# Down products of a transformer block by Strassen's rule, with keys read twice into short rings

## The chip, the cores and the metric

The kernel runs on one core of a Trainium2 chip. Its engines are PE (TensorE, matrix products into PSUM, an accumulation memory of eight banks), DVE (VectorE), ACT (ScalarE), POOL (GpSimd, which works on SBUF, the on-chip memory, alone) and SP (SyncE, which issues DMAs). Each works through its own queue in order; semaphores join them. The metric is the time of one execution in microseconds (us) on the device: the median of several runs.

## What is computed

The reference is a gated pair of transformer branches over 2048 tokens of width 576 (float32):

```python
def _A_ref(x, wqkv, wo):                    # 32 heads of 18
    ...
    scores = jnp.einsum("bhqd,bhkd->bhqk", q, k) * (Dh ** -0.5)
    p = _softmax(scores, axis=-1)
    o = jnp.einsum("bhqk,bhkd->bhqd", p, v)
    return (lambda x, *d: x.transpose(*d))(o, 0, 2, 1, 3).reshape(B, S, D) @ wo

def _B_ref(x, w_gate, w_up, w_down):        # hidden width 4608
    return (_gelu(x @ w_gate) * (x @ w_up)) @ w_down

xn = _layernorm(x, axis=-1)
s = _A_ref(xn, A_wqkv, A_wo)
g = _silu(_B_ref(xn, B_w_gate, B_w_up, B_w_down))
return x + s * g
```

## The kernel before

**Numbers.** Most products are made of float32 operands cut into a high part (rounded to fp32r) and a low part (the rest), with three terms: high x high, high x low, low x high. `split` (L105) cuts on POOL: one one-input operation for the high part, one two-input operation for the low part.

**Stages.** A prologue normalizes x, projects q, k and v and stores them to DRAM (`qk`, `vs`). Then the feed-forward branch runs with the attention woven in; an epilogue ends the feed-forward branch and makes the output projection.

**Feed-forward.** Tokens come in 4 blocks of 512, the hidden width in 36 tiles of 128. One `section` (L644) makes gate and up of one hidden tile for one token block: 27 pairs of matmuls (`gate_up`, L488), gate in the upper and up in the lower 64 rows of the array, then `activate` (L508) makes the hidden tile from the two PSUM banks `pg`, `pu` (ACT: a square, a copy, a tanh; DVE: three operations, the last one `rest`), and `finish` (L692) splits it on POOL. Two sections are a **round** (r of 18 in a block): after its second section the down weights of the two tiles are split too (`dh`, `dl`), and in the next section's tail `downs` (L686) makes the round's down products.

**Down products.** 512 tokens are 4 tiles of 128, 576 columns are 2 halves of 288: eight sums of 2 hidden tiles x 3 terms = 6 products of 128 rows each. In the attention stage `half_downs` (L570) makes each as two products of 64 rows, the upper and the lower half side by side as pairs, in an order written out by hand over eight banks. `add_down` (L542) adds each finished sum to `Y` on DVE. In the last rounds (L633) the products use 128 rows.

**Attention.** A unit is 4 heads by 512 queries: 32 units, 4 sections each. The scores are computed twice: first for the maxima (`max_mm`, L805, reduced by DVE), 40 slots ahead, then for the exponentials (`score_mm`, L858, ACT). Each section has 8 slots of two pairs (`slot_pairs`, L874), spread between its gate and up pairs. After each second section `values` (L892) multiplies exponentials by values, so a round of two sections holds one burst of value products. Four small operations of DVE a unit (`max_neg`, L823) and DMAs (`max_rows`, L849) turn the maxima into rows of q. The keys lie in `KS`, a ring of 7 chunks of 512 keys, each with two tiles of two heads; maxima and scores read the same copy. `load_k` (L768) fills a chunk by 12 DMAs of 18 rows. PSUM's eight banks are three rings: `m` (3), `s` (3), `f` (2).

**Weights.** `load_gu` (L122) loads a hidden tile's gate and up weights by two DMAs, `split_gu` (L129) cuts them in three pieces into rings of five (`wh`, `wl`).

**Order.** PE runs in the order of the text. The other engines' orders are laid by a planner, except where `keep_in_program_order` (through `kept`, from the epilogue on) or an ordering edge (`no_sync`) pins them. All DMAs are issued by SP.

Of the kernel before, what the change touches and what calls it, by code (L numbers as in the profile page):

```python
# [17 lines left out]
P = 128  # L18
# [18 lines left out]
KB, VB = 7, 2  # L37
LEAD = NS + SLOTS
G = 2
# [3 lines left out]
ATT = range(len(FIRST), len(FIRST) + NU * NA)  # L43
MROW = 3 * DH
# [25 lines left out]
def kernel(ctx: ExitStack, tc: tile.TileContext, x, wqkv, wo, w_gate, w_up, w_down, out):  # L70
# [32 lines left out]
    low_part, asked, copied = [], [], []  # L103
# [15 lines left out]
    def raw_tile(shape, pool=wts):  # L119
        return pool.tile(shape, F32, name="raw", tag="raw", bufs=2)  # L120

    def load_gu(t, keep=lambda i: i):  # L122

        raw = raw_tile([P, NC, P])
        for a, w in enumerate((w_gate, w_up)):
            keep(nc.sync.dma_start(raw[HR * a:HR * a + HR], w[:, t * P:(t + 1) * P].rearrange("(k p) n -> p k n", p=HR)))
# [9 lines left out]
    def load_xd(b, key=None):  # L136

        xd = [[], []]
        for c in range(0, NC, XG):
            for i in range(2):  # L140
# [3 lines left out]
                if key:  # L144
                    no_sync(asked[0], key, "keys first")
                copied[:] = [nc.gpsimd.tensor_copy(t[HR:P], t[0:HR])]
                xd[i].append(t)
        return xd
# [5 lines left out]
    with tc.tile_pool(name="pro", bufs=1) as pro, tc.tile_pool(name="pps", bufs=1, space=PSUM) as pps:  # L154
        ident = pro.tile([P, P], F32, name="ident")
        make_identity(nc, ident)

        def load_rest(c0, n, keep=lambda i: i):

            raw = raw_tile([P, n])  # L160
# [199 lines left out]
        def split_wo(k):  # L360
            n = min(P, D - k * P)
            raw = raw_tile([P, D])
# [75 lines left out]
        for b in range(NB):  # L438
# [37 lines left out]
    copied.clear()  # L476
    FF = {"w": ahead, "xd": XD, "down": [], "n": 0, "keep": None, "late": [], "marks": False, "between": [], "added": None,
          "Y": ffn.tile([P, TB // P, D], F32, name="Y")}
# [29 lines left out]
    def activate(pg, pu, early):  # L508

        t1 = ffn.tile([P, TB], F32, name="t1", bufs=2)  # L510
        FF["square"] = kept(nc.scalar.activation(t1, pg, AF.Square))
        one = kept(nc.vector.scalar_tensor_tensor(t1, t1, 1.0 / GC, pg, op0=ALU.add, op1=ALU.mult))
# [6 lines left out]
        def times(behind=None, _=None):  # L519
            one = nc.scalar.activation(t2, pu, AF.Copy)  # L520
            if behind:
                no_sync(one, behind, "a mark first")
            two = nc.vector.tensor_tensor(t2, t2, pg, op=ALU.mult)
# [3 lines left out]
        def tanh(behind=None, _=None):  # L527
            one = kept(nc.scalar.activation(t1, t1, AF.Tanh, scale=GC * GS))
# [3 lines left out]
        def rest(_=None, evicted=None):  # L532
            one = kept(nc.vector.scalar_tensor_tensor(t1, t1, 1.0, t2 if early else pg, op0=ALU.add, op1=ALU.mult))  # L533
# [8 lines left out]
    def add_down(b, r, py, Y, j, c):  # L542
# [101 lines left out]
    def section(specials=(), tag="f", raw_d=None, ahead=True):  # L644
# [6 lines left out]
        if g == 0:  # L651
            FF["hs"] = []
# [535 lines left out]
```

## Time and profile before

| | |
|---|---|
| median of 3 runs | 2535.45 us (2535.36 to 2535.55) |
| span of the profiled execution, first to last instruction | 2533.5 us |
| granted TensorE clock, mean | 1.000 |
| PE / DVE / ACT / POOL busy | 2526.7 / 1953.2 / 1562.0 / 1330.1 us |
| HBM read and written | 266.63 and 54.70 MB |

The profile is of one execution; about 2 us of the time lie around its span. Its page gives busy times, the chain of work that ended last, and the costliest groups of instructions as "line engine operation out<-in shapes xcount | busy us, mean ns | idle before". Other views list instructions in order of time ("start us, us, engine line ..."), or of one line with shortest, median and longest duration. "PEld" is the load of weights into the array, "SPq" is SP's issuing of DMAs, which no busy share counts. A shape such as 64*128 beside a matmul tells the rows and columns of the array that it uses.

### The profile page before, as it was taken

The numbers are of one execution on the slowest core, as the hardware profiler recorded it, in microseconds if no ns is written. First come the engines' busy times: TensorE is split into PE (matmuls) and PEld (weight loads), VectorE is DVE, ScalarE is ACT, GpSimd is POOL, SyncE is SP. The second block draws the span as 40 slices with busy tenths as digits, with TensorE's granted clock in tenths as the row PEclk, the third lists the DMA queues.
The fourth block names the chain that finished last, engine by engine and source line by source line (L and its number), as shares of the span: only waits on it lengthen the run. The fifth ranks groups of instructions, "written<-read, shape, count | busy, mean of one in ns | idle before, by whom it ended". The sixth has DMA issues, their size and how long they took to land.

```text
span 2533.5 us, 63814 instructions
## 1 busy us (share of the span) xinstructions
PE 2526.7 (100%) x24196; PEld 2011.3 (79%) x24196; DVE 1953.2 (77%) x3489; ACT 1562.0 (62%) x3099; POOL 1330.1 (53%) x1462
## 2 busy tenths in 40 slices
PE   9999999999999999999999999999999999999999
PEld 8899987777777778777777777777777777777798
DVE  5317988888888888888888888888888888887277
ACT  3223566676666676666766666766667666666622
POOL 4127554445565545544465555455446555555575
PEclk9999999999999999999999999999999999999999
DMA  7876434444464444444465444444447444444493
GB/s 243 284 263 161 103 94 107 110 111 115 102 156 110 108 112 104 110 113 114 113 135 141 106 111 106 110 104 104 116 110 162 104 106 107 110 111 95 113 250 107
DMA packets 397664, 325.54 MB, mean 128 GB/s; under 512 B 117408, under 2 KB 308160, under 8 KB 397360
## 3 DMA queue, kind: packets, MB, share of 16 engines
q1 hardware_dynamic: 397360, 321.47, 50.1%
q8 instruction: 193, 3.16, 0.6%
q14 instruction: 111, 0.91, 0.1%
HBM read 266.63 MB, written 54.70 MB: 127 GB/s over the span
## 4 chain that ended last, share of the span: by engine, by line
PE 100%; DVE 0%; DMA 0%; issue 0%; ACT 0%
PE pg L498 30%; PE py L561 18%; PE acc L901 18%; PE pm L813 9%; PE pe L866 9%; PE po L177 7%; PE pu L498 5%; PE po L1048 2%; PE pt L247 0%; DMA xx<-in_A_x_dram 0%; PE pt L258 0%; PE pt L177 0%; DVE bs L384 0%; DVE xx L213 0%; DVE yy L1055 0%; DVE yy L1056 0%
## 5 line engine op out<-in xcount | busy, mean ns | idle before, releaser
L867 ACT ACTIVATE pT<-pe 128x512 f32<-128x512 f32 x2048 | 1152.7, 598 | 368.8 <-PE pm L813 228.8
L816 DVE TENSOR_REDUCE mx<-pm 128x1 f32<-128x512 f32 x2048 | 1250.2, 680 | 147.7 <-PE pm L813 145.5
L498 PE MATMUL pu<-xd,wh 64*128 64x512 f32 x2592 | 926.9, 390 | 0.0
L498 PE MATMUL pg<-xd,wh 64*128 64x512 f32 x2592 | 925.8, 390 | 0.0
L813 PE MATMUL pm<-KS,q 64*128 64x512 f32 x2048 | 780.4, 388 | 0.0
L866 PE MATMUL pe<-q,KS 64*128 64x512 f32 x2048 | 777.3, 387 | 0.0
L498 PEld LDWEIGHTS pg<-xd,wh 64*128 64x128 f32 x2592 | 477.2, 184 | 111.8 <-POOL wh L106 29.3
L498 PE MATMUL pu<-xd,wl 64*128 64x512 f32 x1296 | 501.6, 387 | 0.0
L498 PE MATMUL pg<-xd,wl 64*128 64x512 f32 x1296 | 501.5, 387 | 0.0
L498 PEld LDWEIGHTS pu<-xd,wh 64*128 64x128 f32 x2592 | 477.3, 184 | 1.0
L901 PE MATMUL acc<-pT,VS 128*32 128x512 f32 x4096 | 452.8, 594 | 0.0
L108 POOL TENSOR_TENSOR wl<-raw,wh 128x384 fp32r<-128x384 f32 x432 | 434.0, 1018 | 14.0
L106 POOL TENSOR_SCALAR hh<-t 128x512 fp32r<-128x512 f32 x129 | 79.7, 618 | 649.8 <-DVE t L533 647.7
L813 PEld LDWEIGHTS pm<-KS,q 64*128 64x128 f32 x2048 | 375.2, 184 | 28.7 <-DVE mx L816 1.9
L866 PEld LDWEIGHTS pe<-q,KS 64*128 64x128 f32 x2048 | 372.5, 184 | 21.6
L901 PEld LDWEIGHTS acc<-pT,VS 128*32 128x32 f32 x4096 | 127.5, 110 | 289.7 <-issue 284.9
L561 PE MATMUL py<-dh,hh 64*128 64x288 f32 (+1 forms) x2240 | 353.5, 293 | 0.0
L561 PE MATMUL py<-dl,hh 64*128 64x288 f32 (+1 forms) x2240 | 352.7, 292 | 0.0
L561 PE MATMUL py<-dh,hl 64*128 64x288 f32 (+1 forms) x2240 | 352.5, 292 | 0.0
L106 POOL TENSOR_SCALAR wh<-raw 128x384 fp32r<-128x384 f32 x432 | 216.5, 513 | 197.8 <-PE pu L498 130.5
L498 PEld LDWEIGHTS pg<-xd,wl 64*128 64x128 f32 x1296 | 238.8, 184 | 31.2
L549 DVE TENSOR_TENSOR Y<-py,Y 128x288 f32<-128x288 f32 x544 | 226.4, 450 | 40.2 <-PE py L561 32.5
(146 smaller groups left out, 3105.4 us busy)
## 6 DMA issues: line engine op xcount, KB each, us to landing
KS<-qk SPq DMA_DIRECT2D x1536, 36.0 KB
raw<-in_B_w_gate_dram SPq DMA_DIRECT2D x144, 288.0 KB
raw<-in_B_w_up_dram SPq DMA_DIRECT2D x144, 288.0 KB
raw<-in_B_w_down_dram SPq DMA_DIRECT2D x67, 576.0 KB
VS<-vs SPq DMA_DIRECT2D x128, 152.0 KB
qk<-t SPq DMA_DIRECT2D x72, 256.0 KB
q<-qk SPq DMA_DIRECT2D x384, 36.0 KB
xx<-in_A_x_dram SPq DMA_DIRECT2D x32, 288.0 KB
```

What stands on the lines that cost most here:

```text
L106: first = nc.gpsimd.tensor_scalar(hi, raw, 1.0, 1.0, op0=ALU.mult, op1=ALU.mult)
L108: low_part[:] = [keep(nc.gpsimd.tensor_tensor(lo, raw, f(hi), op=ALU.subtract))]
L177: nc.tensor.matmul(o, st, m, start=(i == 0), stop=(i == len(TERMS) - 1))
L498: nc.tensor.matmul(o, w[1 + wp][k][rr, c, :], xd[xp][k][rr, c, :], start=(i == 0), stop=(i == len(terms) - 1))
L549: one = FF["added"] = kept(nc.vector.tensor_tensor(yy, py, yy, op=ALU.add))
L561: return nc.tensor.matmul(py, hs[g][a][rr, j * P:(j + 1) * P], wd[w][rr, g, 288 * c:288 * c + 288], start=start, stop=stop)
L813: nc.tensor.matmul(pm, QS[u, r][rr, t * P:(t + 1) * P], KS[(u * NA + c) % KB][r][rr, :], start=True, stop=True)
L816: return nc.vector.tensor_reduce(MX[u][:, 2 * r + a, t, c:c + 1], pm, axis=AX.X, op=ALU.max)
L866: nc.tensor.matmul(pe, KS[(u * NA + c) % KB][r][rr, t * P:(t + 1) * P], QS[u, r][rr, :], start=True, stop=True)
L867: nc.scalar.activation(PT[u, kt][:, 2 * r + a, :], pe, AF.Exp, scale=SCALE)
L901: nc.tensor.matmul(ACC[u][32 * a:32 * a + 32, :], VS[(u * NA + c) % VB][:, v:v + 32], pt[:, a, :], start=first, stop=last, skip_group_chec ...
L1048: nc.tensor.matmul(po, parts_of(b, j)[x_][:, k, :], OW[w][c][k], start=(i == 0), stop=(i == len(OUT) - 1))
```

## The change

In 63 rounds (5 to 67, `SEVEN`) the down products of a round, a product of 512 tokens x 256 hidden by 256 x 576, are made as seven products of blocks of half the size in each direction, by Strassen's rule in Winograd's form. `cut_hidden` and `cut_down` make the sums and differences of blocks and split them, on POOL, with the high parts of four weight blocks on ACT. `seven_downs` makes 7 products x 2 token tiles of 128 = 14 sums of 3 matmuls of 128 rows. The seven results are added up apart over all rounds of a block of tokens (`Y` has 7 places for each token tile); ten of the 14 sums go out on DVE, four on ACT into `TY`, which `add_copied` adds by two operations of DVE at the end of the round's second section. `combine` joins the seven into the four blocks by seven operations of DVE at the end of a block.

The ring of keys becomes two rings of 3 half chunks, `KM` for the maxima and `KS` for the scores, so that each key is read twice; the slots of a section go through the first half chunk and then the second. Gate and up weights come in three pieces of two DMAs, in one ring of six with the low parts; the high parts have a ring of four. Splits are pinned at thirds of a section. A block's transposed x is copied to the lower half on POOL and ACT, half each. The output projection's weights go to places that become free late, and are loaded later. Names that moved (`S3` to `SIDE`), the epilogue's order of splits, `load_wo` and the functions that only lost an argument are left out of the diff below.

```diff
-KB, VB = 7, 2
+KB, VB = 3, 2
 LEAD = NS + SLOTS
+LEAD_K = 2 * LEAD // SLOTS
+UNITS = 6
+NT_GU = 3 * XG
 G = 2
 NR = F // (G * P)
 NF = NB * NR * G
 FIRST = (0, 0) + (5,) * 8
 ATT = range(len(FIRST), len(FIRST) + NU * NA)
+SEVEN = range(ATT.start // G, ATT.stop // G - 1)
+HALF, CW = TB // 2, D // 2
+A12, A22, A11, S3, S2, S1, S4 = range(7)
+B11, B21, B22, T1, T3, T4, T2 = range(7)
+C11, C12, C21, C22, Q1, Q6, Q5 = range(7)
+PRODUCTS = [(S3, T3, C22), (A11, B11, Q1), (A12, B21, C11), (S2, T2, Q6), (A22, T4, C21), (S1, T1, Q5), (S4, B22, C12)]
+SUMS = [(p, t) for q in range(0, 6, 2) for t in range(2) for p in (q, q + 1)] + [(6, 0), (6, 1)]
+COPIED = [1, 3, 5, 7]
...
     def load_gu(t, keep=lambda i: i):
-        raw = raw_tile([P, NC, P])
-        for a, w in enumerate((w_gate, w_up)):
-            keep(nc.sync.dma_start(raw[HR * a:HR * a + HR], w[:, t * P:(t + 1) * P].rearrange("(k p) n -> p k n", p=HR)))
-        return raw, [], []
+        raws = []
+        for k in range(NG):
+            raw = wts.tile([P, XG, P], F32, name="raw", tag="wu", bufs=UNITS)
+            for a, w in enumerate((w_gate, w_up)):
+                keep(nc.sync.dma_start(raw[HR * a:HR * a + HR], w[k * XG * HR:(k + 1) * XG * HR, t * P:(t + 1) * P]
+                                       .rearrange("(k p) n -> p k n", p=HR)))
+            raws.append(raw)
+        return raws, [], []
     def split_gu(w, k, keep=lambda i: i):
-        hi, lo = (wts.tile([P, XG, P], F32R, name=m, bufs=5) for m in ("wh", "wl"))
-        first = split(hi, lo, w[0][:, XG * k:XG * k + XG, :], keep)
+        hi = wts.tile([P, XG, P], F32R, name="wh", bufs=4)
+        lo = wts.tile([P, XG, P], F32R, name="wl", tag="wu", bufs=UNITS)
+        first = split(hi, lo, w[0][k], keep)
         w[1].append(hi)
         w[2].append(lo)
         return first
...
+    def seven_downs(b, r):
+
+        fresh = (b * NR + r == SEVEN.start) or r == 0
+        done = 0
+        while len(FF["rest"]) > 1:
+            FF["rest"].pop(0)()
+        for n, (p, t) in enumerate(SUMS):
+            a, w, to = PRODUCTS[p]
+            py = bank("msmsmsffmsmsms"[n])
+            for i, (x, y) in enumerate(((AH, BH), (AH, BL), (AL, BH))):
+                nc.tensor.matmul(py, x[:, a, t * P:(t + 1) * P], y[:, w, :], start=(i == 0), stop=(i == 2))
+            yy = Y[:, t, to, :]
+            if n in COPIED:
+                keep(nc.scalar.activation(yy if fresh else TY[:, COPIED.index(n), :], py, AF.Copy))
+                continue
+            if r == 0 or fresh and to in (Q1, Q6, Q5):
+                FF["added"] = keep(nc.vector.tensor_copy(yy, py))
+            else:
+                FF["added"] = keep(nc.vector.tensor_tensor(yy, py, yy, op=ALU.add))
+            done += 1
+            if done == 2 and FF["rest"]:
+                FF["rest"].pop(0)()
+            if done in (3, 4) and FF["between"]:
+                keep(FF["between"].pop(0)())
+        if not fresh:
+            FF["after"].append(add_copied)
+        if r == NR - 1 or b * NR + r == SEVEN.stop - 1:
+            FF["after"].append(lambda: combine(b, r))
+
+    def add_copied():
+
+        places = [(SUMS[n][1], PRODUCTS[SUMS[n][0]][2]) for n in COPIED]
+        for t in range(2):
+            at_t = [i for i, (tt, _) in enumerate(places) if tt == t]
+            for i in at_t:
+                assert places[i][1] == places[at_t[0]][1] + at_t.index(i)
+            yy = Y[:, t, places[at_t[0]][1]:places[at_t[-1]][1] + 1, :]
+            low = TY[:, at_t[0]:at_t[-1] + 1:2, :]
+            keep(nc.vector.tensor_tensor(yy, yy, low, op=ALU.add))
+
+    def combine(b, r):
+
+        for to, x, y, op in ((C11, C11, Q1, ALU.add), (Q1, Q1, Q6, ALU.add), (C22, C22, Q1, ALU.add), (C21, C22, C21, ALU.subtract),
+                             (C22, C22, Q5, ALU.add), (Q1, Q1, Q5, ALU.add), (C12, C12, Q1, ALU.add)):
+            keep(nc.vector.tensor_tensor(Y[:, :, to, :], Y[:, :, x, :], Y[:, :, y, :], op=op))
+        if r == NR - 1:
+            store_y(b, range(TB // P))
...
+    def cut_down(k):
+
+        raw = FF["rawd"].rearrange("p g (c n) -> p (g c) n", c=2)
+        b11, b12, b21, b22 = range(4)
+        if k == 0:
+            for to, x, n in ((B11, b11, 1), (B21, b21, 2)):
+                split(BH[:, to:to + n], BL[:, to:to + n], raw[:, x:x + n], keep)
+            for to, x, y in ((b11, b12, b11), (b12, b22, b12), (b22, b22, b11), (b21, b22, b21)):
+                keep(nc.gpsimd.tensor_tensor(raw[:, to], raw[:, x], raw[:, y], op=ALU.subtract))
+        elif k == 1:
+            keep(nc.scalar.activation(BH[:, T1:T2 + 1], raw, AF.Copy))
+        else:
+            keep(nc.gpsimd.tensor_tensor(BL[:, T1:T2 + 1], raw, f(BH)[:, T1:T2 + 1], op=ALU.subtract))
+
+    def cut_hidden(g, h):
+
+        parts = h.rearrange("p (s t) -> p s t", s=2)
+        pool = nc.gpsimd
+        if g == 0:
+            diff = ffn.tile([P, TB], F32, name="t2", bufs=1)[:, 0:HALF]
+            keep(pool.tensor_tensor(diff, parts[:, 0], parts[:, 1], op=ALU.subtract))
+            split(AH[:, S3], AL[:, S3], diff, keep)
+            split(AH[:, A11], AL[:, A11], parts[:, 0], keep)
+        else:
+            h1 = FF["h1"].rearrange("p (s t) -> p s t", s=2)
+            keep(pool.tensor_tensor(h1[:, 1], h1[:, 1], parts[:, 1], op=ALU.add))
+            keep(pool.tensor_tensor(h1[:, 0], h1[:, 1], h1[:, 0], op=ALU.subtract))
+            split(AH[:, A12:A22 + 1], AL[:, A12:A22 + 1], parts, keep)
+            split(AH[:, S2:S1 + 1], AL[:, S2:S1 + 1], h1, keep)
+            keep(pool.tensor_tensor(parts[:, 0], parts[:, 0], h1[:, 0], op=ALU.subtract))
+            split(AH[:, S4], AL[:, S4], parts[:, 0], keep)
+        FF["h1"] = h
...
+        def splits(k):
+            if nxt and ahead:
+                split_gu(nxt, k, pin)
+            if k == 0 and g == G - 1 and seven(n):
+                cut_down(0)
+
+        for k in range(NG - 1):
+            pairs[NT_GU * (k + 1)] = lambda k=k, p=pairs[NT_GU * (k + 1)]: (splits(k), p())
         for p in spread(pairs, specials):
             p()
         if nxt and ahead:
-            split_gu(nxt, NG - 1, kept)
+            split_gu(nxt, NG - 1, pin)
         FF["w"] = nxt
+        copies = [[], []]
         if n + 1 < NF and (n + 1) % (NR * G) == 0:
-            FF["xd"] = load_xd(b + 1, FF["key"])
-        FF["act"], FF["rest"] = activate(pg, pu, n < ATT.stop)
+            FF["xd"], copies = load_xd(b + 1, True)
+            for m in copies[0]:
+                pin(m())
+        FF["act"], FF["rest"] = activate(pg, pu, n < ATT.stop, pin)
         now = FF["down"] and FF["down"][0][-1] < FF["n"]
         if n < ATT.stop and not now:
             run_rest()
+        if g == G - 1 and seven(n):
+            cut_down(1)
+            cut_down(2)
+        for m in copies[1]:
+            pin(m())
+        if g == G - 1:
+            while FF["after"]:
+                FF["after"].pop(0)()
...
-    KT2 = [key.tile([P, 2, TB], F32R, name=f"KS{i}") for i in range(KB)]
-    KS = [[t[:, r] for r in range(2)] for t in KT2]
+    KM, KS = KT2 = [key.tile([P, KB, TB], F32R, name=f"K{m}") for m in "ms"]
...
-        def load_k(n, keep=lambda i: i, rs=(0, 1)):
-
-            u, c = divmod(n, NA)
+        def load_k(n, ring, keep=lambda i: i):
+
+            (u, c), r = divmod(n // 2, NA), n % 2
             if u >= NU:
                 return
             cols = slice(c * TB, (c + 1) * TB)
-            for r in rs:
-                for a in range(2):
-                    kk = f(KS[n % KB][r])[64 * a:64 * a + MROW, :]
-                    h = QD * (u % NQ) + 2 * r + a
-                    rows = slice(D + h * DH, D + (h + 1) * DH)
-                    for n_, i in enumerate((0, 1, 0)):
-                        keep(nc.sync.dma_start(kk[n_ * DH:(n_ + 1) * DH, :], qk[i, rows, cols]))
+            for a in range(2):
+                kk = f(ring)[HR * a:HR * a + MROW, n % KB, :]
+                h = QD * (u % NQ) + 2 * r + a
+                rows = slice(D + h * DH, D + (h + 1) * DH)
+                for n_, i in enumerate((0, 1, 0)):
+                    keep(nc.sync.dma_start(kk[n_ * DH:(n_ + 1) * DH, :], qk[i, rows, cols]))
...
-            new_x = (FF["n"] + 1) % (NR * G) == 0
-            if new_x:
-                load_k(n - 1 + KB, behind_it)
             section([p for s in range(s0, s0 + SLOTS) for p in slot_pairs(s)])
-            if n > 0 and not new_x:
-                load_k(n - 1 + KB)
-            if n > NU * NA - KB:
-                load_wo((n - 1) % KB)
+            for h in range(2 * n + KB, 2 * n + KB + 2):
+                load_k(h, KS)
+                load_k(h + LEAD_K, KM)
+            if n == NU * NA - LEAD_K // 2:
+                load_wo(flat[0], [(0, 0, k) for k in range(NK)])
```

More of the change, by code (lines that the diff above doesn't have):

```diff
@@ L475, with place, down_pair, hidden @@
     asked.clear()
[L476 removed]
     FF = {"w": ahead, "xd": XD, "down": [], "n": 0, "keep": None, "late": [], "marks": False, "between": [], "added": None,
[L478 removed]
+          "after": []}
+    AH, AL = (ffn.tile([P, 7, HALF], F32R, name=m) for m in ("ah", "al"))
+    BH, BL = (ffn.tile([P, 7, CW], F32R, name=m) for m in ("bh", "bl"))
+    Y = ffn.tile([P, 2, 7, CW], F32, name="Y")
+    TY = ffn.tile([P, len(COPIED), CW], F32, name="TY")
+    def place(j, c):
+        return Y[:, j % 2, 2 * (j // 2) + c, :]
+    def down_pair(t):
+        return t.rearrange("p s n -> p (s n)")[:, 0:G * D].rearrange("p (g n) -> p g n", g=G)
+    def hidden(t, i):
+        return t.rearrange("p s t -> p (s t)")[:, TB * i:TB * i + TB]
+    def seven(n):
+        return n // G in SEVEN
+    keep = tc.keep_in_program_order
     mark = const.tile([P, 1], F32, name="mark")
```

190 lines of the change are left out of this document (101 added, 89 removed).

## Prediction

> **What bounds the kernel now.** I read the page's busy shares and its chain first, then the products of PE (TensorE) in order of time, and last the queue that issues the DMAs, which the page's busy shares leave out.
>
> ```profile
> PE 2526.7 (100%) x24196; PEld 2011.3 (79%) x24196; DVE 1953.2 (77%) x3489; ACT 1562.0 (62%) x3099; POOL 1330.1 (53%) x1462
> ...
> PE 100%; DVE 0%; DMA 0%; issue 0%; ACT 0%
> ```
>
> The kernel is bound by PE from end to end: busy 2526.7 of 2533.5 us, and the chain that ended last never leaves it. What the change takes from PE is therefore gained in full, but only until another resource needs longer per round than PE does. The question is how near the others are.
>
> ```profile
> L901 PE MATMUL acc<-pT,VS x4096: 592/592/618, 313.0 to 2405.0; 128*32 128x512 f32 x196
> ```
>
> The attention stage has 64 rounds, each with one burst of the value products of L901, some 7 us long. The bursts begin at 313.0, and the last one near 2398: 2085 / 63 = **33.1 us a round**. One unit of attention is two rounds, 66.2 us.
>
> **What the change takes from PE.** The timeline of PE, one round's down products in the halves of now, with the pair before and the pair after:
>
> ```profile
> 1229.08 0.39 PE L498 MATMUL pg<-xd,wh 64*128 64x512 f32 x1
> ...
> 1229.31 0.29 PE L561 MATMUL py<-dh,hh 64*128 64x288 f32 x2
> ...
> 1235.54 0.30 PE L561 MATMUL py<-dh,hl 64*128 64x288 f32 x2
> 1235.67 0.39 PE L498 MATMUL pg<-xd,wh 64*128 64x512 f32 x1
> ```
>
> 48 pairs of half products take 1235.67 - 1229.31 = 6.36 us, 0.1325 each; going in and out costs nothing, since the neighbours use the same 64-row halves. The new products use all 128 rows. The kernel has that form at its end, between half-row pairs:
>
> ```profile
> 2421.34 0.39 PE L498 MATMUL pg<-xd,wh 64*128 64x512 f32 x1
> ...
> 2421.66 0.40 PE L561 MATMUL py<-dh,hh 128*128 128x288 f32 x1
> 2421.89 0.29 PE L561 MATMUL py<-dl,hh 128*128 128x288 f32 x1
> 2422.03 0.29 PE L561 MATMUL py<-dh,hl 128*128 128x288 f32 x1
> ...
> 2424.81 0.30 PE L561 MATMUL py<-dh,hl 128*128 128x288 f32 x1
> ...
> 2435.77 0.42 PE L1048 MATMUL po<-KS,oh 128*128 128x288 f32 x2
> 2436.13 0.50 PE L498 MATMUL pg<-xd,wh 64*128 64x512 f32 x1
> ...
> 2436.46 0.39 PE L498 MATMUL pg<-xd,wl 64*128 64x512 f32 x1
> ```
>
> From 2422.03 to 2424.81 lie 21 products: 0.132 each, so a full product costs what a pair of halves does. Each change of form costs something: the third product starts 0.69 after the pair at 2421.34, where a pair's 0.23 (1229.08 to 1229.31) and two products would give 0.49, so 0.20 going in. Going out, the second pair starts 0.56 after the last product (2435.90, the second of the row at 2435.77) against 0.13 + 0.23: 0.20 again. New per round: 7 products x 2 token tiles x 3 terms = 42, 42 x 0.132 + 0.40 = 5.95 us. **Gain 0.41 us a round**, half of what six products are worth; over 63 rounds 26 us. The other pairs and the value products keep their number: PE's floor is 33.1 - 0.4 = 32.7 us a round, 65.4 a unit.
>
> **What it adds on SP.** Every DMA of this stage is issued by SP, in order. The rows of the issuing instructions (shortest, median, longest ns), one run of them, and SP's own waits:
>
> ```profile
> L780 SPq DMA_DIRECT2D KS<-qk x1536: 263/314/1723, 193.1 to 2298.9; - x192
> ...
> L126 SPq DMA_DIRECT2D raw<-in_B_w_gate_dram x144: 595/627/1142, 130.2 to 2463.0; - x144
> ...
> L142 SPq DMA_DIRECT2D xd<-xhs x24: 573/588/1624, 87.6 to 1909.6; - x24
> ...
> L787 SPq DMA_DIRECT2D VS<-vs x128: 370/382/913, 248.5 to 2375.8; - x128
> ...
> L802 SPq DMA_DIRECT2D q<-qk x384: 264/315/1512, 195.6 to 2236.6; - x192
> ...
> L855 SPq DMA_DIRECT2D q<-mT x256: 585/591/711, 283.4 to 2339.3; - x128
> ```
>
> ```profile
> 1260.57 2.80 SPq L780 DMA_DIRECT2D KS<-qk  x8
> ```
>
> ```profile
> SPq L780 <- DMA raw<-in_B_w_up_dram: 116.0, 106, 2.9
> ...
> SPq L855 <- DMA mT<-m2t: 27.2, 23, 2.3
> ...
> SPq L713 <- DMA oN<-num: 20.3, 24, 2.7
> ```
>
> Eight key loads in a row take 2.80 us: (2.80 - 0.31) / 7 = 0.36 from one to the next, the median and 0.045 between. I add 0.045 to every median. A unit now issues 48 key loads (17.3 us), 8 gate and up loads (8 x 0.67 = 5.4), 16 for q (x 0.36 = 5.8), 8 of L855 (5.1), 4 of L787 and 2 down loads (6 x 0.43 = 2.6), and 14 short ones of the sums and their reciprocals, for which I take 0.45, between the cheapest row (0.31) and the dearest (0.67): 6.3, bounds 4.3 and 9.4. Sum 42.5 of 66.2 us: SP has no busy figure on the page, but it is 64% taken by issuing alone.
>
> The change makes 96 key loads of 48, since each half chunk of keys is now read into the ring of the maxima and again into that of the scores: + 17.3. It makes 24 weight loads of 8, three pieces for each: a piece is 64 rows by 3 runs, the form of L142's row, so 0.63 each; by L787's row it would be 0.43, by L126's 0.67. 24 x 0.63 = 15.1, + 9.7 (bounds + 4.9 and + 10.7). So SP needs 42.5 + 17.3 + 9.7 = 69.5 us a unit before any wait. The waits on its own round trips (L855 and L713: 47.5 us over 32 units, 1.5 each) stay; those on PE go when SP is late. **71.0 us a unit, 35.5 a round, against PE's 32.7.** The cover that hid the issues is gone: SP is late next.
>
> What is queued behind: keys, weights, q and values leave by one queue in order, and the rings are short. Three half chunks a ring means that the loads asked for after a section are read one and a half sections later at the most, where 7 whole chunks lay before. So once SP is late PE waits at a section's first scores or maxima (L813 and L866 of now) for a key that has not landed, and everything behind follows PE.
>
> **POOL.** Mean ns of one, now:
>
> ```profile
> L108 POOL TENSOR_TENSOR wl<-raw,wh 128x384 fp32r<-128x384 f32 x432 | 434.0, 1018 | 14.0
> L106 POOL TENSOR_SCALAR wh<-raw 128x384 fp32r<-128x384 f32 x432 | 216.5, 513 | 197.8 <-PE pu L498 130.5 <-DMA raw<-in_B_w_up_dram 66.4
> L108 POOL TENSOR_TENSOR dl<-raw,dh 128x1152 fp32r<-128x1152 f32 x64 | 171.2, 2676 | 5.3
> L108 POOL TENSOR_TENSOR hl<-t,hh 128x512 fp32r<-128x512 f32 x129 | 165.8, 1285 | 10.7
> ...
> L106 POOL TENSOR_SCALAR dh<-raw 128x1152 fp32r<-128x1152 f32 x64 | 74.9, 1170 | 0.0
> L723 POOL TENSOR_TENSOR num<-num,rb 72x256 f32<-72x256 f32 x60 | 44.1, 735 | 163.5 <-DMA rb<-rT 118.1 <-DMA q<-zq 29.4 <-issue 15.4
> ```
>
> Between these sizes a two-input operation costs 0.18 + 2.17 n / 1000 us for n columns, a one-input one 0.19 + 0.85 n / 1000. A round now: six weight splits 9.2, the down split 3.8, two hidden splits 3.8, one L723 0.7: 17.5. New: 9.2 and 0.7 stay; cut_down splits 288 and 576 columns and makes four differences of 288 (3.4 + 3.2), and the low part of four blocks at once (2.7; the high part goes to ACT, 1.2 beside its 20 of 33 us); cut_hidden takes 3.0 for the first hidden tile, 7.1 for the second. Sum 29.3, with 0.08 between dependent ones 30.5 of 32.7 us. That fits, with 2 us left. What eats into it are operations of DVE that read two operands of SBUF:
>
> ```profile
> 2447.66 0.75 DVE L506 SCALAR_TENSOR_TENSOR yy<-th,yy 128x576 f32<-128x576 f32 x1
> ...
> 2450.68 2.12 DVE L506 SCALAR_TENSOR_TENSOR yy<-th,yy 128x576 f32<-128x576 f32 x1
> ```
>
> ```profile
> 2450.53 1.65 POOL L108 TENSOR_TENSOR ol<-OT,oh 128x640 fp32r<-128x640 f32 x1
> ```
>
> The same operation takes 0.75 us alone and 2.12 when POOL had begun its own just before: it waits until POOL ends at 2452.18, then runs. The Trainium skill ("SBUF — State Buffer", section "SBUF: two separate sides") says why: such an operation of DVE and one of POOL that reads SBUF take one pair of ports in turn, for the whole instruction. These rows agree. A round of the new kernel has four such on DVE (two `rest`, two of add_copied), 0.7 each: if all stand in POOL's way, POOL needs 33.3 a round, 0.2 more than a round now.
>
> **DVE and ACT.**
>
> ```profile
> L549 DVE TENSOR_TENSOR Y<-py,Y 128x288 f32<-128x288 f32 x544 | 226.4, 450 | 40.2 <-PE py L561 32.5
> ```
>
> ```profile
> 1235.07 1.63 DVE L549 TENSOR_TENSOR Y<-py,Y 128x288 f32<-128x288 f32 x4 [0.34 <-PE py L561]
> 1236.61 9.66 DVE L816 TENSOR_REDUCE mx<-pm 128x1 f32<-128x512 f32 x16
> ```
>
> Ten sums a round go out by DVE and four by ACT, where eight went by DVE: two more at 0.39 ((1.63 - 0.46) / 3) in a phase 0.4 shorter, with two idle stretches of 0.34 to take it up. DVE now frees itself 0.94 after the section's first pair (1235.67 to 1236.61) and will do so some 0.5 later. Three banks of maxima, one every 0.6 us, cover about that; in every other round the row maxima come on top, where I put 0 to 0.4 on PE, 31 times: 0 to 12 us. The seven operations of `combine`, four times in all, each read two operands of SBUF: 7 x 0.75 = 5 us alone; in turn with as many of POOL of 0.5 to 2.7 us up to 16. The value products cover some 5, so a block end costs PE 0 to 11 us, 0 to 44 in all. While SP is late both hide in its lateness, as SP goes on issuing; I cost them at nothing there, and in full where SP keeps up. The epilogue's weights, loaded later, I put at -5 to +5.
>
> The ring of six pieces lets a split start only when a third of the section has freed its place; two thirds, some 6.5 us, and the down or value products lie before its use, and a split takes 1.6: nothing, unless POOL is late. The bytes:
>
> ```profile
> q1 hardware_dynamic: 397360, 321.47, 50.1%
> ```
>
> 1536 key loads more of 18 x 2 KB are 55 MB: 59% of the DMA engines' time for 50%. Nothing, by the same share.
>
> **The sum.** The ring of the maxima ends five sections before the stage does, so SP binds some 60 rounds: 60 x (35.5 - 33.1) = + 144 us. 2533.5 + 144 = 2677 us of span, and 2 us lie around it (median 2535.45): **2680 us**.
>
> **Rivals.** (a) *SP keeps up and PE stays the bound: faster.* If key loads come at the shortest row (0.31) and pieces at L787's price (0.43), SP needs 96 x 0.31 + 24 x 0.43 + 19.8 + 1.5 = 61.4 a unit, under PE's 65.4; the point from which it decides is 65.4. Then 2535.5 - 26 = 2510, up to 2525 with the row maxima's rounds, if `combine` hides. For it: a quarter of SP's time has been waiting, not issuing. Against: the medians. The Trainium skill ("DMA: Bandwidth & Descriptors", section "Issuing engines are not separate DMA queues") is on this side, in that it holds the time to start a DMA to be usually small beside the DMA itself; by that rule (a) is the outcome. The rows of SP speak against it here, with 0.36 us for each of 166 issues and more.
>
> (b) *POOL is the bound.* SP between 61 and 66 a unit, POOL at 33.3 with its port lost to DVE, and `combine` in full: 2535.5 + 63 x 0.2 + 44 = 2592.
>
> (c) *They cancel.* SP at 66 a unit (pieces at 0.43 and the rest as forecast): within 5 us of now.
>
> (d) Worse than forecast: SP also keeps its waits behind the weights' DMAs (116.0 us in the row above, 3.6 a unit): 74.6 a unit, 37.3 a round, 2788.
>
> **How the numbers follow.** Forecast with (d): 0.55, of which 0.08 for (d) and beyond; (b) 0.13; (c) 0.07; (a) 0.25. A measurement of this kernel can tell some 0.2%, 5 us. Faster 0.25, same 0.07, slower 0.68. Both signs hold much: the forecast's own range is 2600 to 2790, and the range for 8 in 10 reaches down to (a), 2512, and up to 2780.
>
> **What would show it.** In the changed profile: PE's busy share falls to some 94%, and its idle stretches end with key DMAs; the round is 35 to 36 us; SP's key loads follow one another at 0.36 with hardly a wait on PE; a weight piece takes 0.58. Down products of a round take 5.95 us, with 0.2 at either side. POOL is busy near 30 us a round. If PE stays at 100% with rounds of 32.7, my price of an issue is wrong; if PE waits for POOL's splits or for DVE's `combine`, it is (b).

## The result, and the profile after

The changed kernel takes **2989.51 us** (median of 4 runs, 2977.77 to 2992.22) where the kernel before takes 2535.5: ratio 1.178, interval 1.176 to 1.1802. The forecast was 2680, with 2512 to 2780 as its range. It is slower, as forecast, but by 454 us and not by 144.

The page of the changed kernel:

```profile
span 2988.7 us, 62161 instructions
...
PE 2671.7 (89%) x20794; PEld 2061.8 (69%) x20794; DVE 2176.2 (73%) x3758; ACT 1653.7 (55%) x3043; POOL 2129.4 (71%) x2520
...
q1 hardware_dynamic: 448784, 378.19, 44.1%
...
PE 63%; SPq 11%; DMA 11%; POOL 6%; issue 3%; DVE 3%; ACT 2%; POOLq 0%; ACTq 0%; DVEq 0%
```

Two things are to be seen. PE has 3402 products fewer than before and is yet busy 145 us longer; and it stands idle for 2988.7 - 2671.7 = 317 us, before for 7. The chain that ended last was PE alone; now SP's issuing (SPq) and DMAs take 22% of it. The DMA engines are not fuller, for 56.7 MB more: 44.1% of a longer span, where it was 50.1%.

The value bursts, in the changed kernel's rows (their first and last start):

```profile
L1050 PE MATMUL acc<-pT,VS x4096: 592/592/618, 332.6 to 2857.9; 128*32 128x512 f32 x196
```

The first burst comes 19.6 us later than before (313.0). The last begins at 2851.4, so a round takes 2518.8 / 63 = 40.0 us on average. That mean has two kinds of rounds in it. The six at the three block ends inside the stage take 45 and 52 us by turns, 290.5 together; the other rounds, called ordinary here (47, without the first, the last three and the neighbours of a block end), take 39.4 us, where the kernel before has 33.2 in all.

SP in a stretch of the changed kernel (start, time, instruction):

```profile
1309.07 2.07 SPq L921 DMA_DIRECT2D Ks<-qk  x6
1311.18 2.11 SPq L921 DMA_DIRECT2D Km<-qk  x6
1313.38 0.35 SPq L988 DMA_DIRECT2D mT<-m2t  x1
1315.63 0.58 SPq L1085 DMA_DIRECT2D rT<-sums  x1
1316.31 0.61 SPq L139 DMA_DIRECT2D raw<-in_B_w_gate_dram  x1
...
1320.71 0.55 SPq L767 DMA_DIRECT2D wr<-in_B_w_down_dram  x1
1321.37 2.13 SPq L921 DMA_DIRECT2D Ks<-qk  x6
1323.54 3.08 SPq L921 DMA_DIRECT2D Km<-qk  x6
1326.72 3.04 SPq L921 DMA_DIRECT2D Ks<-qk  x6
1329.80 2.12 SPq L921 DMA_DIRECT2D Km<-qk  x6
1331.96 0.32 SPq L859 DMA_DIRECT2D num<-oT  x1
1332.32 0.69 SPq L860 DMA_DIRECT2D rb<-rT  x1
1333.06 5.06 SPq L1004 DMA_DIRECT2D q<-mT  x8
```

and PE at the end of that stretch:

```profile
1331.20 0.50 PE L537 MATMUL pu<-xd,wh 64*128 64x512 f32 x1
1335.85 0.47 PE L1015 MATMUL pe<-q,Ks 64*128 64x512 f32 x1 [4.15 <-DMA q<-mT]
```

SP hardly stops. The row maxima are stored at 1313.38 (mT) and are to be read back into the queries by L1004; but that comes after 24 keys, weights and the sums' numbers in the one queue, so its first DMA leaves at 1333.06, and PE waits 4.15 us for it. No buffer is short here and no transfer is long: the DMA was issued late. The waits of the whole run (sum, times, longest):

```profile
ACT bh L726 <- POOL wr L724: 402.2, 50, 14.3
...
POOL bh L117 <- DMA wr<-in_B_w_down_dram: 223.3, 61, 4.9
...
PE pe L1015 <- DMA q<-mT: 171.5, 32, 16.7
...
PE pm L962 <- ACT accs L1053: 89.3, 27, 5.2
```

The third row is the case just seen. The others make a second chain, read from the second row to the first and on to the last: the down weights' DMA (L767) is late, POOL's cuts wait for it, ACT stands before the cut of the four differences (L726), and what ACT holds back behind it is the eviction of the values (L1053), for which PE waits. 171.5 + 89.3 of PE's 317 idle us stand in these two rows.

Where PE goes on after such a wait it is slow, which is how it can be busy longer with less to do. Windows of the changed kernel around the wait above (busy time of PE, PEld, DVE, ACT, POOL with the number of instructions, then the granted clock, the DMA engines' share and GB/s):

```profile
1331.30:1335.80 4.50, 0.40 (x2) 0.08 (x2) 0.69 (x1) 1.16 (x1) 4.18 (x6) 1.00 0.22 69
1335.80:1336.90 1.10, 1.05 (x7) 0.76 (x7) 0.42 (x1) 0.48 (x1) 1.10 (x2) 0.90 0.02 3
1336.90:1340.90 4.00, 4.00 (x24) 3.44 (x24) 2.40 (x5) 2.26 (x5) 3.88 (x4) 0.60 0.15 36
1342.00:1346.00 4.00, 4.00 (x38) 3.67 (x36) 3.97 (x8) 3.63 (x8) 3.75 (x6) 1.00 0.67 177
```

About one microsecond after the wait the granted clock falls: its mean over the next 4 us is 0.60, and they hold 24 products where 38 go through at full clock.

### The profile page after: what moved, and what is told of

It reads as the page before. It is cut to its first block, busy times and chain, and to the rows that moved or that the text cites. A ratio compares the mean times of both kernels' runs of the same rounds, so it can differ in the third digit from the quotient of the medians.

```text
span 2988.7 us, 62161 instructions
## 1 busy us (share of the span) xinstructions
PE 2671.7 (89%) x20794; PEld 2061.8 (69%) x20794; DVE 2176.2 (73%) x3758; ACT 1653.7 (55%) x3043; POOL 2129.4 (71%) x2520
## 2 busy tenths in 40 slices
DMA packets 449100, 382.16 MB, mean 128 GB/s; under 512 B 140544, under 2 KB 332576, under 8 KB 448784
## 3 DMA queue, kind: packets, MB, share of 16 engines
q1 hardware_dynamic: 448784, 378.19, 44.1%
## 4 chain that ended last, share of the span: by engine, by line
PE 63%; SPq 11%; DMA 11%; POOL 6%; issue 3%; DVE 3%; ACT 2%; POOLq 0%; ACTq 0%; DVEq 0%
PE pg L537 14%; PE py L673 11%; PE pu L537 10%; SPq L921 8%; PE pe L1015 8%; PE pm L962 7%; DMA wr<-in_B_w_down_dram 6%; PE po L199 6%; PE acc L1050 2%; DMA q<-mT 2%; PE po L1194 2%; PE py L602 2%; DMA Ks<-qk 1%; POOL wr L724 1%; ACT pT L1016 1%
## 5 line engine op out<-in xcount | busy, mean ns | idle before, releaser
L537 PE MATMUL pg<-xd,wh 64*128 64x512 f32 x2592 | 996.4, 418 | 9.4 <-POOL wh L117 9.4
L1015 PE MATMUL pe<-q,Ks 64*128 64x512 f32 x2048 | 827.3, 416 | 173.5 <-DMA q<-mT 171.5
L962 PE MATMUL pm<-Km,q 64*128 64x512 f32 x2048 | 827.8, 419 | 90.2 <-ACT accs L1053 89.3
L1015 PEld LDWEIGHTS pe<-q,Ks 64*128 64x128 f32 x2048 | 402.9, 199 | 224.2 <-DMA q<-mT 117.0
L962 PEld LDWEIGHTS pm<-Km,q 64*128 64x128 f32 x2048 | 404.4, 200 | 139.3 <-ACT accs L1053 100.7
L726 ACT ACTIVATE bh<-wr 128x1152 fp32r<-128x1152 f32 x63 | 73.3, 1163 | 506.1 <-POOL wr L724 402.2
L119 POOL TENSOR_TENSOR al<-t,ah 128x256 fp32r<-128x256 f32 (+1 forms) x318 | 306.8, 965 | 26.5
L673 PE MATMUL py<-bh,ah 128*128 128x288 f32 x882 | 271.4, 308 | 5.7 <-DVE t L564 2.7
L537 PEld LDWEIGHTS pg<-xd,wl 64*128 64x128 f32 x1296 | 257.2, 198 | 22.8 <-POOL wl L119 0.8
L537 PEld LDWEIGHTS pu<-xd,wl 64*128 64x128 f32 x1296 | 256.2, 198 | 11.9
L673 PE MATMUL py<-bl,ah 128*128 128x288 f32 x882 | 261.0, 296 | 0.0
```

The lines of the kernel that those rows point to most:

```text
L119: low_part[:] = [keep(nc.gpsimd.tensor_tensor(lo, raw, f(hi), op=ALU.subtract))]
L537: nc.tensor.matmul(o, w[1 + wp][k][rr, c, :], xd[xp][k][rr, c, :], start=(i == 0), stop=(i == len(terms) - 1))
L673: nc.tensor.matmul(py, x[:, a, t * P:(t + 1) * P], y[:, w, :], start=(i == 0), stop=(i == 2))
L726: keep(nc.scalar.activation(BH[:, T1:T2 + 1], raw, AF.Copy))
L962: nc.tensor.matmul(pm, QS[u, r][rr, t * P:(t + 1) * P], keys(KM, u, c, r)[rr, :], start=True, stop=True)
L1015: nc.tensor.matmul(pe, keys(KS, u, c, r)[rr, t * P:(t + 1) * P], QS[u, r][rr, :], start=True, stop=True)
```

## The experiments

**SP's load taken off, in three ways.** The theory: the time of a round is SP's. The first takes away the second reading of the keys:

```diff
                 load_k(h, KS)
-                load_k(h + LEAD_K, KM)
```

The maxima are then taken over keys that lie in the ring from before: the subtracted maxima are not those of the scores.

> The changed kernel without the second reading of keys: the ring of the maxima is filled three times over in the lead and then kept as it is, so the maxima after that are taken over other keys (left out: 48 key loads a unit and their bytes). SP's issuing falls from 75.5 to about 57.7 us a unit, under the 65.4 that PE needs. If SP's issuing binds: rounds of 33 to 35 us instead of 40, time 2560 to 2680. If POOL and its port, or DVE, bind: the rounds stay at 38 to 40, time 2900 to 2990. If the DMA engines' bytes bind: also faster, since 55 MB go; the next two tell that apart.

Measured 2620.66 us, ratio 1.0335 (1.0305 to 1.0365).

The second leaves the keys and loads gate and up by two DMAs a hidden tile, as before (one raw buffer, a ring of three for the low parts):

```diff
-        for k in range(NG):
-            raw = wts.tile([P, XG, P], F32, name="raw", tag="wu", bufs=UNITS)
+        raw = wts.tile([P, NC, P], F32, name="raw", bufs=1)
+        for a, w in enumerate((w_gate, w_up)):
+            keep(nc.sync.dma_start(raw[HR * a:HR * a + HR], w[:, t * P:(t + 1) * P].rearrange("(k p) n -> p k n", p=HR)))
```

> The changed kernel with the gate and up weights of a hidden tile loaded by two DMAs, not six; the same bytes, the same splits on POOL. SP's issuing falls by 16 DMAs of 0.63 to 0.68 us and 8 get 0.05 dearer: 75.5 to 64.5 us a unit, about at PE's 65.4. If SP's issuing binds: rounds of 34 to 37 us, time 2620 to 2800. If bytes, POOL or DVE bind: 2950 to 3000.

Measured 2882.8 us, ratio 1.1369 (1.1277 to 1.146): between the two ranges, and 107 us gained where at least 190 were expected.

The third stores queries and keys in DRAM with their three parts side by side, so that the 54 rows of a head come by one DMA and not three. The bytes read in the stage are the same:

```diff
-    qk = dram.tile([2, 2 * D, S], F32, name="qk")
+    qk = dram.tile([2 * D, 3, S], F32, name="qk")
...
-                for n_, i in enumerate((0, 1, 0)):
-                    keep(nc.sync.dma_start(kk[n_ * DH:(n_ + 1) * DH, :], qk[i, rows, cols]))
+                keep(nc.sync.dma_start(kk, qk[rows, :, cols].rearrange("d i t -> (d i) t")))
```

> The changed kernel with q and keys stored in DRAM as three planes beside each other (high, low and once more high for keys), so that the 54 rows of a key or query tile come by one DMA instead of three; the same bytes read, 9 MB more written by 44 more DMAs in the prologue. SP issues 32 key loads a unit instead of 96 and 8 for q instead of 16: 75.5 to about 49.5 us. If SP's issuing binds: it is wholly under PE's need, rounds of 33 to 35 us, time 2550 to 2680. If bytes bind: 2980 to 3020. If POOL or DVE bind: 2900 to 2990.

Measured 2633.77 us, ratio 1.0386 (1.0356 to 1.0417). Its page:

```profile
PE 2546.3 (97%) x20794; PEld 1920.7 (73%) x20794; DVE 2202.7 (84%) x3758; ACT 1659.0 (63%) x3043; POOL 2149.3 (82%) x2520
...
q1 hardware_dynamic: 433424, 387.54, 50.4%
...
PE 83%; DVE 9%; DMA 3%; POOL 2%; issue 1%; SPq 0%; ACT 0%; POOLq 0%; DVEq 0%; ACTq 0%
```

SP has left the chain, and 356 us are gone, with more bytes (387.54 MB), nearly as many packets (433424 for 448784) and the DMA engines as full as before the change. So neither bytes nor packets were the bound. PE makes the same 20794 products in 125 us less, at a mean granted clock of 0.984 where the changed kernel has 0.941: so much of the changed kernel's loss is its clock.

**SP's load put on, without the change.** The kernel before, with each key load cut in two halves of its columns (the first run), and also each gate and up load cut in three (the second). Not a byte more is read, and nothing else is changed:

```diff
-                        keep(nc.sync.dma_start(kk[n_ * DH:(n_ + 1) * DH, :], qk[i, rows, cols]))
+                        for x in range(2):
+                            xx = slice(c * TB + x * (TB // 2), c * TB + (x + 1) * (TB // 2))
+                            keep(nc.sync.dma_start(kk[n_ * DH:(n_ + 1) * DH, x * (TB // 2):(x + 1) * (TB // 2)], qk[i, rows, xx]))
```

> The kernel before with its key loads alone cut in column halves: 48 more DMA issues a unit, the same bytes, no Strassen products, gate and up weights by two DMAs as before. By the run with 64 more issues SP's time for them is about 32 to 33 us of each round of 33.1: at the knee. Queue theory (nothing is lost until SP's queue is full, then all of it): 2545 to 2750. Rival (each added DMA costs PE its share whether the queue is full or not, 434 us for 27 us of issues a unit): 48 issues by 0.36 = 17.3 us a unit, 17.3 / 27 of 434 = 278, so 2790 to 2840.

> The kernel before with more DMAs for the same bytes and nothing else changed: each key load cut into two of half the columns (96 a unit for 48) and the weights of a hidden tile loaded by six DMAs for two. No Strassen, no more work on POOL, DVE or ACT. SP's issuing rises from 46.9 to about 74 us a unit, as in the changed kernel. If SP's issuing binds: rounds of 37 to 40 us for 33.1, time 2780 to 2990. If POOL, DVE, bytes or the new down products cost the time: 2535 to 2560.

Measured 2796.01 us for the keys alone, ratio 1.1026 (1.1004 to 1.1048), and 2969.25 for both, ratio 1.1709 (1.1675 to 1.1743). The page of the latter:

```profile
PE 2693.7 (91%) x24196; PEld 2135.5 (72%) x24196; DVE 2014.8 (68%) x3489; ACT 1554.9 (52%) x3099; POOL 1360.5 (46%) x1462
...
q1 hardware_dynamic: 448048, 321.56, 38.8%
...
PE 68%; SPq 13%; DMA 11%; DVE 4%; issue 3%; ACT 1%; POOL 0%; ACTq 0%; POOLq 0%
```

As many issues of keys and weights as the change makes, and nothing of Strassen's rule, give nearly the changed kernel's time. The keys alone missed the range of the queue theory (up to 2750) and hit that of its rival, a price for each DMA whether SP is full or not. The kernels together decide between the two. SP's time is here the sum of its instructions in an ordinary round, with up to 0.06 us between one and the next, from the trace (good to some 0.2 us):

| kernel | SP's time a round | SP's waits for landings | ordinary round | PE idle, whole run |
|---|---|---|---|---|
| before | 22.8 us | 4.6 us | 33.2 us | 7 us |
| changed, one DMA a key | 24.4 | 2.5 | 33.2 | 83 |
| changed, no second reading | 29.0 | 1.8 | 33.2 | 67 |
| changed, whole weights | 31.7 | 5.2 | 37.4 | 254 |
| before, keys in halves | 32.0 | 4.6 | 36.6 | 166 |
| changed | 37.3 | 1.7 | 39.4 | 317 |
| before, keys and weights cut | 37.7 | 1.9 | 39.5 | 275 |

Up to 29 us of 33 nothing is lost in an ordinary round, so there is no price for each DMA. Between 29 and 32 the queue becomes the bound, before its own time fills the round: that is 85 to 95% of the longer rounds. The third column has the rest. In the traces every DMA names one of eight semaphores, in turn, and is issued only when that semaphore tells that the eighth DMA before it has landed; the queue serves in order, so those behind it wait too. A key load waits in this way for a large load of weights that it never reads. The two columns together make 27 to 31 us in the first three kernels, where SP spends the rest of the round waiting for other engines, and 36.6 to 39.6 in the last four, which is their round within 0.5 us.

So the queue theory was right in kind, and set its knee too late, since it left these waits out; the whole weights missed their range by the same term. This is read from the traces: no run has more semaphores and all else as it was.

**The same DMAs from another queue.** In the changed kernel the loads of queries and values (the first run) or the second reading of the keys (the second) are issued by ACT (`nc.scalar.dma_start` for `nc.sync.dma_start`).

> The changed kernel itself, with the loads of queries, their zero rows and the values issued by ScalarE in the place of SyncE: the same DMAs, the same bytes. About 8.4 us of the 75.5 us of issues a unit leave SP's queue (67 left, 33.5 a round). If SP's issuing is the bound: 2780 to 2900. If the DMA engines or the memory behind them are: 2965 to 3010, as the changed kernel.

> The changed kernel itself, with the second reading of the keys (48 loads a unit, for the row maxima) issued by ScalarE: the same DMAs, the same bytes, and 17.7 us of issues a unit leave SP's queue (57.8 left, as many as in the run without these loads, which took 2620.7). If SP's issuing is the bound: 2620 to 2720, the more the longer ScalarE stands before a full ring. If the transfers are the bound: 2965 to 3010.

Measured 3142.64 us, ratio 1.2394 (1.2369 to 1.2419), and 3300.15, ratio 1.3015 (1.2989 to 1.3041): both expectations fell. In the first, SP's time fell to 33.3 us a round, but both queues take the same eight semaphores in turn: SP waits 8.4 us a round for landings, mostly of the values and queries that ACT issues, and the two make its ordinary round of 41.9. In the second, SP's time fell to 28.5 us a round, as meant, but the ordinary round rose to 44.9. Its waits:

```profile
PE py L673 <- ACT t L561: 302.6, 60, 9.0
...
ACT t L561 <- DMA Km<-qk: 234.5, 37, 9.9
```

ACT's sequencer now stands before key loads, and its work waits behind them: the copy of L561, and behind that PE's down products. The second run says what a blocking DMA costs on a computing engine. Neither run took DMAs from SP without a new wait, so they do not decide between SP and the transfers, and the case rests on the others.

**What is left: block ends and start.** The kernel with one DMA a key has the old ordinary round and is yet 98 us slower. Its windows of two ordinary rounds, of the two at the first block end, and of 4 us within the first of these (columns as above):

```profile
593.50:626.50 33.00, 32.37 (x278) 23.38 (x274) 30.54 (x55) 23.55 (x44) 28.81 (x36) 1.00 0.40 116
626.50:660.20 33.70, 33.70 (x290) 23.80 (x286) 31.71 (x53) 24.70 (x46) 30.12 (x36) 1.00 0.52 153
727.00:774.00 47.00, 36.12 (x286) 25.23 (x282) 31.07 (x56) 28.69 (x48) 36.61 (x43) 0.85 0.62 145
774.00:818.50 44.50, 35.86 (x286) 25.20 (x282) 42.56 (x59) 24.03 (x45) 33.69 (x38) 0.88 0.46 143
746.50:750.50 4.00, 3.45 (x16) 2.79 (x18) 1.77 (x3) 3.16 (x6) 3.92 (x4) 0.50 0.79 185
```

DVE is at 31 and POOL at 29 to 30 us of a round of 33. In the second round of the block end DVE has 11 us more, which is `combine`, and is the bound. Left out:

> The changed kernel with one DMA a key, and without the seven sums at a block's end (the block products are not combined, so the output is another). If the sums lie openly on VectorE, three block ends lose 11 to 15 us each against the run with one DMA a key (2633.8): 2588 to 2601. If they are hidden and the block ends are long for another cause, less than 10 us go: 2624 to 2636.

Measured 2601.35 us: 32.4 less, 10.8 a block end, and the second round of an end falls from 44.5 to 32.8. The first did not (46 to 49). The next run tries that round, with the lower half of x loaded by DMA (`asked` is a list of its loads; the line is cut at its end):

```diff
-                    copies[i].append(lambda t=t: nc.scalar.activation(t[HR:P], t[0:HR], AF.Copy))
+                    asked[:] = [nc.sync.dma_start(f(t)[HR:P], xhs[b][i, c * HR:(c + XG) * HR, :]...)]
```

> The changed kernel with one DMA a key, and the lower half of the transposed x at a block's start loaded by six more DMAs in the place of three copies on GpSimd and three on ScalarE. If those copies hold up ScalarE's eviction of the values and GpSimd's weights, the first round of a block end falls from 46.8 to 33 to 36 us, three times: 2592 to 2604. If the wait is for the DMA into the one buffer of x itself, it stays: 2625 to 2640.

Measured 2631.46 us: nothing gained. SP in that round:

```profile
737.53 0.57 SPq L158 DMA_DIRECT2D xd<-xhs  x1
739.13 0.57 SPq L162 DMA_DIRECT2D xd<-xhs  x1
741.05 1.99 SPq L921 DMA_DIRECT2D Ks<-qk  x2
744.46 1.94 SPq L921 DMA_DIRECT2D Km<-qk  x2
```

Behind twelve loads of x of 384 KB each, a key load starts only every 1.7 us, when the x load eight issues before it has landed (a row of two holds the wait between them), and PE now waits for keys (3 times, up to 5.4 us) where it waited up to 8.4 us for an eviction that stood behind ACT's copies of x. So the second case of the expectation holds: that round waits for x's loads. Before the change the same six loads and their copies cost PE nothing. By the text of the kernel there were two covers that are gone, half of a round's down products between the last section of a block and the next, and whole chunks of keys loaded far ahead; that was not tried by itself. The covers are not enough where SP is late: the kernel before with its keys in halves has both, and its first round of a block end takes 49 to 53 us, with this wait at the three ends:

```profile
PE pg L498 <- DMA xd<-xhs: 35.4, 3, 12.9
```

Then the repairs together (x by DMA, `combine` shared between DVE and POOL and half of it behind the values' eviction, row maxima late, weights ahead of the first keys), and the late row maxima alone:

```diff
-            if done in (3, 4) and FF["between"]:
+            if done in (9, 10) and FF["between"]:
```

> The changed kernel with one DMA a key, x by DMA, the seven sums of a block's end shared (four on VectorE, three on GpSimd, half of them behind the values' eviction), the steps of the row maxima behind the round's last sums, and the first keys and queries loaded behind the weights of the second section. By the terms found: 2633.8 less 42 (x), 20 (sums), 19 (0.63 us of every second round) and 5 to 10 (start) = 2543; range 2525 to 2575. Rival: VectorE and GpSimd are full (31 and 29 of 33 us a round), so what is moved comes out elsewhere: 2580 to 2620.

> The changed kernel with one DMA a key (2633.8), the two steps of the row maxima between a round's sums moved behind its last two sums. In that run every second round is 0.9 us longer (33.6 to 32.7), with one gap of 0.6 us before a down product while VectorE is behind. If those two steps are what puts it behind: 0.6 to 0.9 of 30 rounds, 2606 to 2616. If VectorE is simply full in such a round, the time moves elsewhere: 2628 to 2638.

Measured 2643.04 us for all repairs (ratio 1.0429, 1.0412 to 1.0446), outside both ranges and no better than without them, and 2632.25 for the late row maxima (1.0382, 1.0364 to 1.0399). The rival was right about the latter: rounds with row maxima fall from 33.6 to 33.1, and those without rise from 32.7 to 33.0, as a full DVE would have it. With all repairs, the second round of a block end fell by some 3.6 us (to between 40.1 and 41.7), and other rounds rose. No version of the change beat the kernel before, and these numbers say why none is near: with SP free an ordinary round takes what it took before, so block ends and start at no cost at all would bring 2535, not less.

## Why the prediction was wrong in size

**PE's gain: right.** The down products, first and last, with the pair on either side:

```profile
1307.37 0.39 PE L537 MATMUL pu<-xd,wh 64*128 64x512 f32 x1
1307.69 0.40 PE L673 MATMUL py<-bh,ah 128*128 128x288 f32 x1
...
1313.32 0.29 PE L673 MATMUL py<-bh,al 128*128 128x288 f32 x1
1313.54 0.50 PE L537 MATMUL pg<-xd,wh 64*128 64x512 f32 x1
```

Here 5.85 us lie between the first product and the next pair. Measured as the forecast was, from the pair before to the second pair after, the kernel with one DMA a key takes 6.41 us in the rounds without row maxima, where 6.82 was needed before: 0.41 gained, as forecast. With SP free those rounds take 32.73, where the floor was put at 32.7.

**The new bound: right.** SP's issuing, by the runs with issues added and taken away. Rival (a) held that SP would keep up. The Trainium skill's sentence on its side ("DMA: Bandwidth & Descriptors", section "Issuing engines are not separate DMA queues": the time to start a DMA is usually small beside the DMA) is no guide to the outcome here, where more and smaller DMAs of the same bytes made 2969 us of 2535; the measurement decides.

**The sum: wrong, and this is the step that failed: "71.0 us a unit, 35.5 a round".** Ordinary rounds took 39.4, 3.9 more. By SP's time 2.6 of them are issues: 37.3 us a round where 69.5 / 2 = 34.8 was priced. 3.2 us a unit were missing already in the count for now (22.8 x 2 = 45.7, not 42.5), and about 2 in what was added: a weight piece takes its place for 0.68 us, not 0.63, and the semaphore steps between DMAs were left out. The other 1.3 are waits: 2.1 us a round, with 0.75 forecast. The forecast let only the waits on SP's own round trips stay and had those on PE go "when SP is late"; the waits behind weights' DMAs, which rival (d) kept, it left out. They stayed: 1.7 of the 2.1 us are for landings, most of them of the down weights, before which key loads stand 78.8 us in the whole run, SP's largest wait. Over 60 rounds 3.9 us make 234. The range was also narrower than its own rivals: it ended at 2780, and (d) stood at 2788.

**`combine` and block ends: wrong.** "While SP is late both hide in its lateness ... I cost them at nothing there." In the changed kernel the six rounds at block ends take 290.5 - 6 x 39.4 = 54 us more than ordinary ones, 18 an end. The bounds for `combine` alone, 0 to 11 us, hold what it measures with one DMA a key (10.8), at their far end. In the changed kernel it does not hide, because SP does not go on issuing: SP itself stores the finished blocks, and stands before those stores until `combine` is done. The second round of the first block end:

```profile
841.24 1.76 SPq L921 DMA_DIRECT2D Ks<-qk  x5
848.04 3.80 SPq L713 DMA_DIRECT2D ys<-Y  x4
...
862.81 0.76 PE L1015 MATMUL pe<-q,Ks 64*128 64x512 f32 x1 [16.71 <-DMA q<-mT]
```

SP stands still for 5 us and is then 3.8 us at the four stores, 2 of them waiting again; the row maxima's loads come later still, and PE waits 16.6 to 16.7 us for them in this round of each of the three ends. That is read from the trace; no run leaves `combine` out while SP is late. In the first round of each end PE waits 7 to 9 us for POOL's copy of x; x's load was not in the sum. And the start of the stage was not: 19.6 us. The weights of the third section are asked for behind the first keys and queries (issued from 204.9 us on, before from 187.0), and PE waits 7.8 us for their split. That they are the whole of it is not shown: with all repairs, where those keys come behind the weights, this wait is 0.5 us and the first burst still begins at 330.7, 17.7 later than before.

The three make 234 + 54 + 20 = 308 of the 312 us between the forecast's span of 2677 and 2988.7.

**What would show it: half right.** Key loads follow at 0.36 (six in 2.1 us), as said; a weight piece takes 0.61, where 0.58 was said. PE is at 89%, not 94, and its idle stretches end mostly with the returning row maxima and a held-up eviction, not with keys. Seen from PE and not from SP, the missing term has another name: the forecast had PE at full clock between its waits, and 125 of the 360 us of span between this kernel and the one with a DMA a key are the same products at a lower clock.

POOL was priced well: 30.5 us a round forecast, 28.8 and 30.1 in the windows of the kernel with one DMA a key. DVE was not summed over a round; at 31 of 33 us it is what eats the gain in every second round.

## What to carry to other kernels

Count the DMAs of a round and multiply by what one takes on the engine that issues them, and add what that engine waits for earlier DMAs to land, before splitting or repeating loads: this kernel was lost to SP at 0.36 to 0.68 us a DMA while the DMA engines were less than half busy. Here the in-order queue was the bound when its issues took 85 to 95% of the round, as waits for landings filled the rest, and what was late then was what was asked for last and needed first: the small DMAs of a round trip. When an edit uses up the slack of several engines at once (here SP 37, DVE 31 and POOL 29 us for a round of 33), a gain of 1% on the bound has nowhere to appear, and each rare piece of work, such as a block's end, shows in full.

## What was not expected of the hardware

A wait costs PE more than its length. In the rows above PE waited 4.15 us and then ran 4 us at a mean granted clock of 0.60 (0.50 from 1336.7 to 1340.1), which is about 1.6 us more. In the run with one DMA a key, 746.5 to 750.5 us behind a wait of 8.4 us, it was 0.50 throughout. Over the whole run the changed kernel's PE is busy 2671.7 us and that other one's 2546.3, for the same products. The kernel before shows it too: 2526.7 us, and 2693.7 for the same 24196 products with keys and weights cut. The Trainium skill ("TensorE: Matmul & The Clock Gate", section "Part 1: The HAM clock gate (the "warmup" mystery)") says that PE falls to half its clock after an idle window of about 3.4 us and returns after a busy one. The spell's length, 3.4 us, agrees, and here the fall came 1 us after PE had resumed.

And SP can be held up by what has long been issued. With x by DMA a key load takes SP 0.27 us behind the twelve loads of x as elsewhere, but one leaves only every 1.7 us, because the loads of x, 384 KB each, land at that pace and each issue waits for the eighth before it.
